# Four buffers for the dense output's transposed tiles, and their logits five planned microseconds later

## The chip, the cores and the metric

The kernel runs on one NeuronCore of a Trainium2 chip. The metric is the device time of one execution in microseconds (us). The core has five engines that each work through a list of their own in order: TensorE (PE, whose weight loads are shown as PEld), VectorE (DVE), ScalarE (ACT), GpSimd (POOL) and SyncE (SP), which issues most of the DMAs.

## What is computed

The reference is a chain of three layers over 3072 tokens (4 batches of 768) with 320 features:

```python
# 1. a recurrent attention over time (4 batches, 8 heads, 768 steps, 40 wide), with stabilised gates
C = f_stab * C + i_stab * outer(v_t, k_t);  n = f_stab * n + i_stab * k_t
y[:, :, t] = sigmoid(o_gate_t) * (C @ q_t) / max(|n . q_t|, 1)
# 2. a dense layer, 320 -> 2048 -> 320
h = x @ w_in;  g = maximum(0.01 * h, h);  x = g @ w_out
# 3. one expert of eight for each token, 320 -> 1024 -> 320
logits = x @ w_gate;  e_idx = argmax(logits)
eom = sigmoid(x @ w_output_gate)
out[mask] = gate_w * eom[e] * (maximum(x[mask] @ w1[e], 0) @ w2[e])
```

## The kernel before

Attention is done in 24 units (6 chunks of 128 time steps by 4 batches). A unit makes one tile of 128 tokens; two units make a pair, so there are 12 pairs. A pair's tokens go through the dense layer in eight steps of `gemm1` (PE line L870, 16 matmuls), an evaluation on three engines (`t` on ACT, `g` on DVE, `gh` on ACT, `gl` on POOL) and, two steps later, `gemm2` (L892 to L894, 12 matmuls). After a pair's last `gemm2`, `finish` copies or adds the accumulators into float32 rows and starts `x2out` for each of the two tiles.

`x2out` is what the change touches. It packs the float32 rows into two float16 halves (`x2r`, by ACT and DVE), writes them to DRAM (`x2rows`, SP line L902), has a DMA transpose them into a tile `x2T` (SP line L904), and then computes the tile's router logits: eight small matmuls `lp<-wg,x2T` (PE, L915) and a copy to `Lall` on ACT. The tiles are numbered 0 to 23; tile i belongs to batch b = i mod 4. Tiles 0 to 19 (pairs 0 to 9, `bufs` given, called part A in the code, `TA = 20`) take this way; the logits of tiles 20 to 23 are kept in `late` and computed later, among the expert blocks. `x2T` has two buffers in the pool `dp`.

The order on each engine is not the order of the code. Every piece of work is a generator that is started at a planned time; `yield 3.0` in `x2out` puts the logits' planned time three microseconds behind that of the transpose. `Order.run` then goes through all instructions with a cost model of its own, gives each engine the ready instruction with the lowest planned time, and fixes that order (for planned times up to 350). So a planned time sets a place in a list, and nothing at run time waits for a clock: at run time an instruction starts when those ahead of it on its engine have started and what it reads is there.

The arena is one large tile that holds other data in each stage. Its region `R3`, 5120 float16 columns, holds `X2F` (float32 rows of the dense output), `YR` (L769's product of queries and state, scaled on DVE and added to `o1` on DVE) and `X32`. Later, the second weight of expert 3 is put into the same columns.

After the dense layer, part A's logits are routed (a long chain on DVE), tokens are gathered into blocks of 128, and the blocks run through the experts (L1177 and L1196) to the end.

Of the kernel before, what the change touches and what calls it, by code (L numbers as in the profile page):

```python
# [9 lines left out]
F16 = mybir.dt.float16  # L10
# [9 lines left out]
B, H, S, D = 4, 8, 768, 40  # L20
# [9 lines left out]
TA = 2 * PF  # L30
# [3 lines left out]
D1 = D + 1  # L34
# [45 lines left out]
class Order:  # L80
# [62 lines left out]
    def run(self, instrs, planned, pools):  # L143
# [57 lines left out]
        def enter(i):  # L201
            q = ops[i]
            t = ready_t[i]
            if q.engine == E.SP:
                t = max(t, prio[i] - DMALEAD)
            heapq.heappush(wait[q.engine], (t, i))
# [6 lines left out]
        while n < len(ops):  # L213
# [11 lines left out]
            if not avail[e]:  # L225
                free[e] = t
                continue
            if e == E.SP and dma_free > t + DMAQ:
                free[e] = dma_free - DMAQ + 0.001
                continue  # L230
# [113 lines left out]

CHAINT = 350
DMALEAD = 2
DMAQ = 10


def emit(tc, gates, qkv, og, w_in, w_out, w_gate, w1, w2, out):  # L350
# [11 lines left out]
    def tt(eng, o, a, b, op):  # L362
        eng.tensor_tensor(out=o, in0=a, in1=b, op=op)  # L363
# [7 lines left out]
    def copy(o, a, s=1.0):  # L371
        A.activation(out=o, in_=a, func=AF.Copy, scale=s)  # L372
# [65 lines left out]
    dp = Slots(tc.alloc_tile_pool(name="dp", bufs=2), 2)  # L438
# [102 lines left out]
    R3 = Region(3 * 5120, 4 * 5120)  # L541
# [11 lines left out]
    CH = Bufs([cp.tile([104, H, 42], F16, name="ch"), R.f16(H, 42, p=104)], "CH")  # L553
    CL = Bufs([R.f16(H, 42, p=104) for _ in range(2)], "CL")
    C3 = [R.f16(H, 42) for _ in range(B)]
    YR = Bufs([R3.f32(H, D1) for _ in range(2)], "YR")
    X32 = Bufs([R3.f32(H, D) for _ in range(2)], "X32")
    SG = Bufs([R.f32(B, DM) for _ in range(2)], "SG")
    for t in CH.items + CL.items:
# [125 lines left out]
    def unit(i):  # L685
# [78 lines left out]
        if c > 0:  # L764
            assert C3[b] is None or ver[b] == c, (i, ver)
            yr = YR()
            o2 = ps.tile([128, H, D1], F32, tag="aux", name="o2", bufs=3)
# [5 lines left out]
            tt(V, o1, o1, yr, ALU.add)  # L773
            YR.free(yr)
        else:
# [61 lines left out]
    def pack(xr, x, s, pool=False):  # L837
        dup = lambda a: a.unsqueeze(1).to_broadcast([128, 2, 64])
        v2 = lambda a: a.rearrange("p (u d) -> p u d", u=2)
        copy(xr[:, 0:256], x[:, 0:256], s)  # L840
        copy(v2(xr[:, 512:640]), dup(x[:, 256:320]), s)
        for o, a, hi in ((xr[:, 256:512], x[:, 0:256], xr[:, 0:256]),
                         (v2(xr[:, 640:768]), dup(x[:, 256:320]), v2(xr[:, 512:640]))):
            if pool:
                less(True, o, a, hi)
            else:
                low(o, a, s, hi)
# [48 lines left out]
    def x2out(acc, c, b, bufs, tag="aux"):  # L896
        i = c * B + b
        xr = dp.tile([128, 768], F16, tag="x2r", name="x2r")
        pack(xr, acc, S_X2 / (S_X * S_WIN * S_WOUT))
        if bufs:  # L900
            bufs.free(acc)
        SP.dma_start(x2rows[i * 128:(i + 1) * 128, :], xr)  # L902
        x2T = dp.tile([128, 6, 128], F16, tag="x2T", name="x2T")
        SP.dma_start_transpose(out=x2T, in_=xr)  # L904
        if bufs:
            yield 3.0
            logits(i, x2T, tag)
        else:
            late.append((i, x2T, tag))

    def logits(i, x2T, tag):
        lp = ps.tile([128, 16], F32, tag=tag, name="lp", bufs=NB[tag])
        with tc.high_priority():
            for m, (xb, wb) in enumerate(X_MOVES):
                T.matmul(lp, x2T[:, xb, :], wg[:, wb, :], start=(m == 0), stop=(m == 7))  # L915
            copy(Lall[:, i, :], lp)
# [345 lines left out]
    def finish(p, kp):  # L1262
        for i in range(2):
            a = acc[p][i]
            if p < 4 and kp == 3:
                if i:
                    V.tensor_copy(part[p][i], a)
                else:
                    copy(part[p][i], a)
                continue  # L1270
            if p < PF:
                x = X2F()
                if p < 4:
                    tt(V, x, a, part[p][i], ALU.add)
                elif i:
                    V.tensor_copy(x, a)
                else:
                    copy(x, a)
                a = x
            at(now + 0.5 + 0.1 * i, x2out(a, *pairs[p][i], X2F if p < PF else None))  # L1280
        del acc[p]
# [94 lines left out]
def build(arrays):  # L1376
    import concourse.bacc as bacc

    nc = bacc.Bacc("TRN2", target_bir_lowering=False, num_devices=1)
    args = [nc.dram_tensor(n, a.shape, mybir.dt.from_np(a.dtype), kind="ExternalInput").ap()  # L1380
            for n, a in arrays.items()]
    args.append(nc.dram_tensor("out", (NT, DM), F32, kind="ExternalOutput").ap())
    with tile.TileContext(nc, schedule_with_timeline_sim=True) as tc:
        emit(tc, *args)
    return nc
# [9 lines left out]
```

## Time and profile before

| what | us |
|---|---|
| median of 3 runs | 690.59 (687.31 to 693.65) |
| the profiled execution's own time | 690.56 |
| its span, first to last instruction | 688.8 |
| PE busy in the span | 618.6 |

The profiled execution is as long as the median run, and 1.8 us of it lie outside the span. An engine's busy time says how much of the span its instructions cover; the idle time in front of an instruction is put down to whatever released it.

### The profile page before, as it was taken

The numbers are of one execution on the slowest core, as the hardware profiler recorded it, in microseconds if no ns is written. First come the engines' busy times: TensorE is split into PE (matmuls) and PEld (weight loads), VectorE is DVE, ScalarE is ACT, GpSimd is POOL, SyncE is SP. The second block draws the span as 40 slices with busy tenths as digits, with TensorE's granted clock in tenths as the row PEclk, the third lists the DMA queues.
The fourth block names the chain that finished last, engine by engine and source line by source line (L and its number), as shares of the span: only waits on it lengthen the run. The fifth ranks groups of instructions, "written<-read, shape, count | busy, mean of one in ns | idle before, by whom it ended". The sixth has DMA issues, their size and how long they took to land. (4 is left out here: it accounts for less than half of the span.)

```text
span 688.8 us, 14711 instructions
## 1 busy us (share of the span) xinstructions
PE 618.6 (90%) x5276; PEld 460.0 (67%) x5276; DVE 396.5 (58%) x766; ACT 353.8 (51%) x736; POOL 316.7 (46%) x342
## 2 busy tenths in 40 slices
PE   3658999888999899989989999999789999999993
PEld 1547687676777787878878877777445655665652
DVE  6795689935575656754757655698435722222220
ACT  4643584598566588685845665654432222222220
POOL 5483796646375555555444542324513522222211
PEclk9995899999999999999999999999999999999997
DMA  8865494763779886997484665734899878868842
GB/s 243 264 159 148 144 255 131 243 186 60 157 190 211 174 224 172 254 201 198 122 172 129 167 168 155 183 109 127 210 198 170 163 158 164 156 138 153 168 95 53
DMA packets 213793, 116.67 MB, mean 169 GB/s; under 512 B 168727, under 2 KB 201239, under 8 KB 213720
## 3 DMA queue, kind: packets, MB, share of 16 engines
q1 hardware_dynamic: 210808, 106.64, 66.5%
q0 software_dynamic: 2912, 9.05, 4.9%
q8 instruction: 47, 0.77, 0.5%
q14 instruction: 26, 0.21, 0.1%
HBM read 64.54 MB, written 9.06 MB: 107 GB/s over the span
## 5 line engine op out<-in xcount | busy, mean ns | idle before, releaser
L870 PE MATMUL hp<-xT,arena 128*128 128x256 f16 x1536 | 192.4, 276 | 2.6 <-DVE g L363 2.1
L363 POOL TENSOR_TENSOR gl<-g,gh 128x512 f16<-128x512 f32 x96 | 122.5, 1276 | 135.4 <-ACT gh L372 133.8
L870 PEld LDWEIGHTS <-arena 128*128 128x128 f16 x1536 | 148.8, 99 | 25.0 <-issue 4.0
L892 PE MATMUL acc<-arena,gh 128*128 128x320 f16 x384 | 115.6, 302 | 3.5 <-ACT arena L372 2.4
L894 PE MATMUL acc<-arena,gl 128*128 128x320 f16 x384 | 115.6, 303 | 2.3 <-POOL gl L363 2.3
L893 PE MATMUL acc<-arena,gh 128*128 128x320 f16 x384 | 115.7, 302 | 0.7 <-POOL arena L363 0.7
L360 DVE SCALAR_TENSOR_TENSOR r<-hp,r 128x512 f16<-128x512 f32 x52 | 35.7, 691 | 110.3 <-ACT r L1183 94.9
L1177 PE MATMUL hp<-arena,xbb 128*128 (+1 forms) x480 | 95.6, 381 | 2.9 <-DVE g L363 1.1
L363 DVE TENSOR_TENSOR g<-hp,t 128x512 f32<-128x512 f32 x96 | 65.7, 685 | 49.1 <-ACT t L372 39.3
L1196 PE MATMUL y<-arena,rT 128*128 (+1 forms) x720 | 90.3, 299 | 2.6 <-DMA rT<-r 2.6
L372 ACT ACTIVATE gh<-g 128x512 f16<-128x512 f32 x96 | 60.0, 625 | 46.7 <-DVE g L363 46.1
L1196 PEld LDWEIGHTS <-rT 128*128 128x128 f16 (+1 forms) x720 | 61.9, 101 | 29.7 <-DMA rT<-r 3.7
L360 DVE SCALAR_TENSOR_TENSOR arena<-stg,arena 128x960 f16<-128x960 f32 (+3 forms) x48 | 59.6, 1244 | 32.0 <-ACT arena L372 30.7
L372 ACT ACTIVATE t<-hp 128x512 f32<-128x512 f32 x96 | 56.3, 586 | 39.1 <-PE hp L870 38.8
L1177 PEld LDWEIGHTS <-xbb 128*128 128x128 f16 (+1 forms) x480 | 41.5, 101 | 47.9 <-issue 4.8
L1200 POOL DMA_INDIRECT out<-ys,si x26 | 26.8, 1033 | 88.4 <-ACT ys L1199 71.9
L372 ACT ACTIVATE arena<-arena 128x640 f16<-128x640 f32 (+4 forms) x73 | 49.2, 688 | 33.6 <-DVE arena L360 14.8
L360 DVE SCALAR_TENSOR_TENSOR arena<-arena 128x320 f16<-128x320 f32 (+4 forms) x64 | 54.6, 860 | 17.3 <-ACT arena L372 16.7
L1183 ACT ACTIVATE r<-hp 128x512 f16<-128x512 f32 x52 | 30.8, 598 | 52.8 <-PE hp L1177 44.3
L372 ACT ACTIVATE arena<-stg 128x1024 f16<-128x1024 f32 (+2 forms) x48 | 46.9, 979 | 19.7 <-DMA stg<-w 17.8
L1199 ACT ACTIVATE ys<-y,ss 128x320 f32<-128x320 f32 x26 | 13.7, 527 | 77.0 <-PE y L1196 68.1
L759 PE MATMUL o<-arena 128*128 128x41 f32 x384 | 52.8, 301 | 0.0
(240 smaller groups left out, 810.3 us busy)
## 6 DMA issues: line engine op xcount, KB each, us to landing
stg<-w SPq DMA_DIRECT2D x24, 512.0 KB
arena<-qkv SPq DMA_DIRECT2D x24, 484.0 KB
arena<-gd SPq DMA_DIRECT2D x18, 512.0 KB
stg<-w SPq DMA_DIRECT2D x16, 480.0 KB
raw<-w_in SPq DMA_DIRECT2D x10, 512.0 KB
arena<-w_out SPq DMA_DIRECT2D x8, 640.0 KB
x2rows<-x2r SPq DMA_DIRECT2D x24, 192.0 KB
arena<-og SPq DMA_DIRECT2D x6, 640.0 KB
```

Of the source, the lines that this page charges most:

```text
L360: eng.scalar_tensor_tensor(out=o, in0=a, scalar=s, in1=b, op0=op0, op1=op1)
L363: eng.tensor_tensor(out=o, in0=a, in1=b, op=op)
L372: A.activation(out=o, in_=a, func=AF.Copy, scale=s)
L759: T.matmul(o1[:, h, :], gm[:, h, :], v[:, h, :], start=True, stop=True)
L870: T.matmul(hp[:, kk, :], win_v[:, j, wb, o:o + 128], xT[:, xb, :], start=(m == 0), stop=(m == 7))
L892: T.matmul(acc[i], gh[:, kk, r], wh, start=(k == lo), stop=False)
L893: T.matmul(acc[i], gh[:, kk, r], wl, start=False, stop=False)
L894: T.matmul(acc[i], gl[:, kk, r], wh, start=False, stop=(k == hi))
L1177: T.matmul(hp[n][r], xT[:, xb, r], W1v[:, e, wb, n * 512:(n + 1) * 512].rearrange("p a b -> p (a b)"), start=(m == 0), stop=(m == 7))
L1183: A.activation(out=r[:, 0, :], in_=hp[n], func=AF.Relu)
L1196: T.matmul(y[r], a[:, r], W2v[:, e, k, m, :].rearrange("p a b -> p (a b)"), start=(k + n == 0), stop=(k == 7 and n == 2))
L1200: G.indirect_dma_start(out=out, out_offset=bass.IndirectOffsetOnAxis(ap=D_[s][1][:, i:i + 1], axis=0), in_=ys, in_offset=None, bounds_chec ...
```

## The change

The logits of tiles 0 to 17 get a planned time 8 us behind the transpose in place of 3 us; tiles 18 and 19, the last pair of part A, keep 3 us. Every tile with an odd batch now takes its transposed tile from two buffers in the arena (`X2T`), the others from the two of the pool, so that there are four in all. To make room in `R3`, `YR` goes from two buffers to one.

```diff
 CHAINT = 350
 DMALEAD = 2
+
+LOGD = 8.0
 DMAQ = 10
...
-    YR = Bufs([R3.f32(H, D1) for _ in range(2)], "YR")
+    YR = Bufs([R3.f32(H, D1)], "YR")
+    X2T = Bufs([R3.f16(6, 128) for _ in range(2)], "X2T")
...
-        x2T = dp.tile([128, 6, 128], F16, tag="x2T", name="x2T")
+        mine = bufs and b % 2
+        x2T = X2T() if mine else dp.tile([128, 6, 128], F16, tag="x2T", name="x2T")
         SP.dma_start_transpose(out=x2T, in_=xr)
         if bufs:
-            yield 3.0
+
+            yield 3.0 if i >= TA - 2 else LOGD
             logits(i, x2T, tag)
+            if mine:
+                X2T.free(x2T)
```

What this does to the order is shown at three places. In the rows, L915 and L922 are the same line before and after (logits); so are L892 to L894 and L895 to L897 (`gemm2`), L870 and L873 (`gemm1`), L751 and L754 (`sc`, a unit's scores), L759 and L762 (`o1`), L769 and L772 (`o2`), L902 and L905 (rows to DRAM), L904 and L908 (the transposes), L722 and L725 (transposes of a unit's queries and keys), L809 to L811 and L812 to L814 (a unit's state).

On PE at tile 12, before: the logits stand inside a `gemm2`, behind its seventh matmul.

```order
L894 LDWEIGHTS gl
L894 MATMUL acc<-arena,gl 128x320
L892 LDWEIGHTS gh
L892 MATMUL acc<-arena,gh 128x320
L915 LDWEIGHTS x2T
L915 MATMUL lp<-wg,x2T 128x16
...
L893 LDWEIGHTS gh
L893 MATMUL acc<-arena,gh 128x320
```

On PE at tile 12, after:

```order
L896 LDWEIGHTS gh
L896 MATMUL acc<-arena,gh 128x320
L897 LDWEIGHTS gl
L897 MATMUL acc<-arena,gl 128x320
L754 LDWEIGHTS arena
L754 MATMUL sc<-arena 128x128
...
L922 LDWEIGHTS x2T
L922 MATMUL lp<-wg,x2T 128x16
...
L873 LDWEIGHTS arena
```

The logits of tile 12 now stand behind the whole `gemm2` (five matmuls more) and behind four score matmuls of a unit.

On SP at tiles 12 and 13, before: the transpose of tile 13 stands behind four state copies.

```order
L902 DMA x2rows<-x2r 128x768
L904 DMA_TRANSPOSE x2T<-x2r 128x6x128
L902 DMA x2rows<-x2r 128x768
L809 DMA arena<-arena 40x336
L810 DMA arena<-arena 40x336
L811 DMA arena<-arena 40x336
L809 DMA arena<-arena 40x336
L904 DMA_TRANSPOSE x2T<-x2r 128x6x128
```

On SP at tiles 12 and 13, after:

```order
L905 DMA x2rows<-x2r 128x768
L908 DMA_TRANSPOSE x2T<-x2r 128x6x128
L905 DMA x2rows<-x2r 128x768
L908 DMA_TRANSPOSE arena<-x2r 128x6x128
L812 DMA arena<-arena 40x336
L813 DMA arena<-arena 40x336
L814 DMA arena<-arena 40x336
L812 DMA arena<-arena 40x336
```

The odd tile's transpose, now into the arena, stands ahead of the state copies.

On PE at tile 0, before: its logits follow the 14th matmul of a `gemm1`.

```order
L870 LDWEIGHTS arena
L870 MATMUL hp<-xT,arena 128x256
L915 LDWEIGHTS x2T
L915 MATMUL lp<-wg,x2T 128x16
...
L870 LDWEIGHTS arena
L870 MATMUL hp<-xT,arena 128x256
...
L892 LDWEIGHTS gh
L892 MATMUL acc<-arena,gh 128x320
```

On PE at tile 0, after:

```order
L897 LDWEIGHTS gl
L897 MATMUL acc<-arena,gl 128x320
L762 MATMUL o_1805<-arena 128x41 x8
L772 LDWEIGHTS arena
L772 MATMUL o_1894<-arena 128x41
...
L922 LDWEIGHTS x2T
L922 MATMUL lp<-wg,x2T 128x16
```

The rest of that `gemm1`, a whole `gemm2` and a unit's `o1` and `o2` now stand ahead of them.

## Rows read from the trace of the kernel before

**Rows 1.** The page: PE's busy time, and the granted clock in 40 slices (tenths).

```profile
PE 618.6 (90%) x5276; PEld 460.0 (67%) x5276; DVE 396.5 (58%) x766; ACT 353.8 (51%) x736; POOL 316.7 (46%) x342
...
PEclk9995899999999999999999999999999999999997
```

**Rows 2.** Busy time by stretch: PE, PEld, DVE, ACT, POOL; clock; DMA share, GB/s.

```profile
160.00:200.00 40.00, 34.96 (x361) 28.48 (x359) 24.73 (x45) 26.63 (x70) 21.99 (x23) 1.00 0.69 152
...
280.00:320.00 40.00, 38.27 (x418) 32.58 (x418) 24.98 (x53) 29.85 (x68) 22.14 (x26) 1.00 0.85 214
...
440.00:480.00 40.00, 38.05 (x332) 29.98 (x331) 34.12 (x79) 20.25 (x34) 14.15 (x11) 1.00 0.45 125
480.00:520.00 40.00, 32.98 (x211) 18.51 (x209) 17.09 (x34) 15.53 (x33) 13.40 (x11) 0.96 0.95 202
```

**Rows 3.** Waits, whole span: us in total, times, longest.

```profile
PE lp L915 <- DMA x2T<-x2r: 14.4, 14, 1.8
...
ACT Lall L372 <- PE lp L915: 7.2, 11, 1.9
```

**Rows 4.** Waits of PE between 160 and 440 us, all of them.

```profile
PE lp L915 <- DMA x2T<-x2r: 13.5, 13, 1.8
PE sc L751 <- DVE arena L363: 2.4, 3, 1.4
PE hp L870 <- DVE g L363: 0.5, 1, 0.5
```

**Rows 5.** Timeline of PE around tile 12's logits: start, us, instruction [idle before].

```profile
344.94 0.30 PE L894 MATMUL acc<-arena,gl 128*128 128x320 f16 x1
345.08 0.30 PE L892 MATMUL acc<-arena,gh 128*128 128x320 f16 x1
...
345.49 0.30 PE L892 MATMUL acc<-arena,gh 128*128 128x320 f16 x1
347.60 0.36 PE L915 MATMUL lp<-wg,x2T 128*128 128x16 f16 x8 [1.81 <-DMA x2T<-x2r]
```

**Rows 6.** Timeline of PE: tile 0's logits, a dense gemm1, a unit's o1.

```profile
168.67 0.36 PE L915 MATMUL lp<-wg,x2T 128*128 128x16 f16 x8 [1.08 <-DMA x2T<-x2r]
...
181.50 1.91 PE L870 MATMUL hp<-xT,arena 128*128 128x256 f16 x16
...
184.88 1.88 PE L759 MATMUL o<-arena 128*128 128x41 f32 x16
```

**Rows 7.** Timeline of SP, the transpose of tile 0.

```profile
165.84 1.25 SPq L904 DMA_TRANSPOSE x2T<-x2r  x1
```

**Rows 8.** Timeline of SP, the transposes of tiles 12 and 13.

```profile
341.70 1.37 SPq L904 DMA_TRANSPOSE x2T<-x2r  x1
343.16 0.55 SPq L902 DMA_DIRECT2D x2rows<-x2r  x1
...
348.11 1.23 SPq L904 DMA_TRANSPOSE x2T<-x2r  x1
```

**Rows 9.** Timeline of POOL, the `gl` of the gemm2 at 344.7 us.

```profile
337.83 1.16 POOL L363 TENSOR_TENSOR gl<-g,gh 128x512 f16<-128x512 f32 x1 [0.80 <-ACT gh L372]
```

**Rows 10.** Busy time by stretch (columns as in group 2), around a clock drop.

```profile
236.00:242.00 6.00, 6.00 (x46) 4.84 (x47) 2.42 (x7) 0.78 (x2) 2.02 (x2) 0.72 0.65 130
342.00:348.00 6.00, 4.19 (x50) 3.29 (x49) 5.55 (x9) 3.26 (x6) 1.40 (x2) 1.00 0.91 196
```

**Rows 11.** Timeline of PE, tile 7's logits and what follows.

```profile
235.63 0.36 PE L915 MATMUL lp<-wg,x2T 128*128 128x16 f16 x8 [0.69 <-DMA x2T<-x2r]
...
237.91 3.35 PE L870 MATMUL hp<-xT,arena 128*128 128x256 f16 x15
```

**Rows 12.** Waits of PE between 440 and 520 us, the longest.

```profile
PE acc L894 <- POOL gl L363: 2.1, 2, 1.8
```

**Rows 13.** Timeline of PE around tile 19's logits.

```profile
442.23 0.60 PE L870 MATMUL hp<-xT,arena 128*128 128x256 f16 x4
443.72 0.36 PE L915 MATMUL lp<-wg,x2T 128*128 128x16 f16 x8 [0.89 <-DMA x2T<-x2r]
```

## Prediction

> **What bounds the kernel now.** I read the page first: PE is busy for 618.6 of 688.8 us, far above any other engine, and its clock is granted in full almost everywhere behind the start [rows 1]. The table of stretches then shows three stages [rows 2]. From 160 to 440 us the dense layer and the attention units share the core, with PE busy for 35 to 39 of each 40 us and DVE and ACT for 25 to 31. From about 445 us DVE's routing chain is the tighter one (34.1 of 40 us). Behind 480 us the expert blocks start with some idle time. A busy PE tells how full it is but not what its idle time is worth, so the third view is the list of waits. Over the whole span its longest row on PE is the router's logits waiting for the DMA that transposes their tile: 14 waits, 14.4 us, the longest 1.8 [rows 3]. Between 160 and 440 us there is hardly anything else: 13 of these waits with 13.5 us, against 2.4 and 0.5 us for the two other reasons [rows 4]. PE takes its matmuls in order, so whatever stands behind the logits waits too.
>
> **The waits, priced.** At tile 12 [rows 5] the `gemm2` matmuls follow each other every 0.14 us (344.94 to 345.08), then the logits come 1.81 us behind the end of the last. The view counts idle time from the end of a matmul, which lasts 0.30 us although the next could have started 0.14 us behind its start. So a wait costs the idle time plus about 0.17 us (0.16 behind `gemm2`; 0.17 behind `gemm1`, whose 16 matmuls take 1.91 us, so 0.11 each [rows 6] with an end 0.28 behind the start). In all: 14.4 + 14 x 0.17 = 16.8 us. Tile 19's wait, 0.89 + 0.16 = 1.05 us [rows 13], belongs to a tile whose planned time stays. **15.75 us** are within the change's reach.
>
> Why they wait: a transpose is not there soon. Tile 0's is issued at 165.84 [rows 7] and its logits start at 168.67 [rows 6], 2.8 us later; tile 12's takes from 341.70 [rows 8] to 347.60 [rows 5], 5.9 us. These are the shortest kind and the longest. [...]
>
> **What the later planned time does.** It does not add 5 us; it moves the logits back in PE's list, and the order shows by how much. I priced the matmuls that now stand between the old place and the new with the spacings above (`gemm1` 0.11, `gemm2` 0.14; a unit's `o1` 1.88 for 16 [rows 6], so 1.7 until the next can start; a unit's scores and `o2` follow one another still closer and make under 0.25 us of any entry). For tiles 0 to 17 this gives 3.8, 4.5, 1.9, 1.4, 0.8, 1.5, 2.6, 1.7, 1.7, 2.6, 2.5, 2.5, 0.9, 0.95, 2.3, 3.0, 1.1 and 1.6 us. The waits to be covered, priced as above, are 1.2, 1.35, 0.8, 0.9, 0.2, 1.0, 1.3, 0.85, 1.9, 0.75, 1.9, 0, 2.0, 0, 0, 0, 0.4 and 1.2 us. Each is covered but two: tile 8 keeps 0.15 and tile 12 keeps 1.1 us. Tile 19's logits come five `gemm1` matmuls earlier in the list (0.55 us), while its transpose comes one SP instruction sooner; I take 0.3 us, between 0 and 0.55.
>
> The two added buffers and the lost one: the transposes of odd tiles write to the arena and stand earlier on SP. At 13 the transpose was issued at 348.11, 4.95 us behind the write of its rows at 343.16 [rows 8], because four state copies stood between; now it goes first and the copies come 1.3 us later (1.23 us of SP, plus a gap). No wait of PE between 160 and 440 us is for a unit's state or for its transposed queries and keys [rows 4], so these had time to spare, how much the list does not tell; I take 0, at most 1.3 us for each of the nine odd tiles below 18. `YR` with one buffer orders the next unit's scaled product behind this unit's addition. Both are on DVE, which takes them in this order anyway: 0. The second expert weight that later lands on `X2T` is converted behind tile 19's logits in both orders: 0.
>
> **Does something else take the waits' place?** What PE waits for next is the evaluation chain (ACT, DVE, ACT, POOL). The `gl` that the `gemm2` at 344.7 us reads ended at 337.83 + 1.16 = 338.99 [rows 9], 5.95 us ahead of its first use at 344.94 [rows 5], and read in the same way, the lead of most other steps is 2 to 7 us. Removing 1 or 2 us ahead of a step eats into that lead but not through it, and the other engines gain too: ACT idles for 7.2 us for these same logits [rows 3]. Behind 440 us everything hangs on what PE has finished (the logits of tile 19 start DVE's routing, the last `gemm2` frees the columns for the last weights), so the whole rest moves forward by what was saved.
>
> Sum: 15.75 - 0.15 - 1.1 - 0.3 = **14.2 us**, against the profiled execution's own 690.56: 676.4. That execution is as long as the median of the three runs (690.59), so no correction: **676 us**.
>
> **The clock.** Once in the stage, just behind tile 7's logits, the granted clock falls to the lower level, 1.2 GHz: the mean from 236 to 242 us is 0.72 [rows 10], and 15 `gemm1` matmuls take 3.35 us [rows 11] where 16 take 1.91. That is 1.6 us. Just ahead of it PE had waited for tile 7's logits (0.69 us) [rows 11]. Around the longest wait, at tile 12, the clock stays at 2.4 GHz (1.00 from 342 to 348 us) [rows 10], so one wait does not bring it on, and I leave the 1.6 us out of the sum and put it into the low end.
>
> **The rivals.**
> - *The moved transposes bite.* SP is a list too: with odd tiles first, the transposes of queries and keys, and the state copies, are issued 1.3 us later. If none of that is covered, PE waits for scores or `o2`: 9 x 1.3 = 11.7 us come back, 688 us. For it: scores already wait three times, 2.4 us. Against: those waits are for DVE, not for a DMA [rows 4].
> - *The stage is paced by DMA, not by PE.* Then PE only gets to the next transfer sooner: about 690 us. For it: a DMA share of 0.85 from 280 to 320 us [rows 2]. Against: in that stage PE waits for no DMA but the logits' [rows 4]. The Trainium skill, in "Perfetto Trace Analysis", section "What "DMA-bound" means", calls a kernel DMA-bound when single DMA engines or the issuing sequencer are at their limit; a mean share of 0.85 over 16 engines neither shows nor excludes that, so this rival keeps a chance.
> - *ACT stops at the copies (slower).* ACT works in order; the copy of the logits to `Lall` now stands elsewhere in its list, and if it stands ahead of the evaluation of a step while PE comes to the logits late, `t` and `gh` are held, and through them `gemm2`. It costs only what exceeds the lead (5.95 us at the step shown). Above 0.8 us beyond the lead at each of the 18 tiles (14.2 / 18) it eats the gain; at 1.3 us it takes 23 us, and the time is 700 us. For it: ACT already idles 11 times for these copies [rows 3]. Against: the order moves the copy together with the matmuls.
> - *It does not do what it says*, since the places in the list move too little. The rows of the order exclude it but for tiles 8 and 12; it is in the sum.
>
> **How the numbers follow.** The forecast has a chance of 0.78, the moved transposes 0.11, the DMA's pace 0.06, ACT's copies 0.05. Low end: 676.4 less 1.6 (clock), less 2 us (the longest wait of PE behind 440 us is 2.1 us [rows 12], in a stretch whose order changes as well), less 1.5 us, half of what the shown runs spread below their median: 671 us. High end: 676.4 plus the same 2 us for the worse, plus 8 of the 11.7 us of the first rival: 686.5 us. A difference of under 1% (6.9 us) is about what a measurement of this kernel cannot tell from no change. Faster by over 1%, below 683.7: the forecast's 0.78 and part of the first rival, 0.80. Within 1%: the rest of the first two rivals, 0.15. Slower: 0.05.
>
> **What would show it.** If right, the row of logits waiting for their DMA shrinks from 14 waits to three or four with under 4 us, PE's other waits between 160 and 440 us stay near 3 us, and tile 19's logits start about 13 us sooner than at 443.72 [rows 13]. If the first rival holds, new PE rows appear for scores or `o2` behind a DMA or DVE. If ACT's copies hold, `gemm2` waits for `gh` or `gl`. I am wrong most cheaply if transposes land even later in the tighter stage, so that 1 us of setback no longer covers tiles 4, 12, 16 and 17.

## The result and the profile after

| | us |
|---|---|
| median of the changed kernel, 20 runs | 682.44 (675.34 to 693.38) |
| median of the kernel before, 20 runs beside them | 687.47 (681.11 to 695.12) |
| ratio, with its 95% interval | 0.9917 (0.9892 to 0.9941) |
| the profiled execution's own time, and its span | 689.69, 688.0 |

The change makes the kernel 5.0 us faster. The forecast was 14 us and a time of 676, so the sign was right, the size was not, and the gain is below the 1% that the forecast gave a chance of 0.80. The forecast's time started from 690.56 us, 3.1 us above the median of the 20 runs before, so it misses the time by 6 us and the gain by 9; that the time looks nearer is luck. The profiled execution of the changed kernel happens to be one of its slow ones (granted clock 0.968 over the span, 0.975 in the one of before), which the ratios here and below leave out, so its own time says nothing on the gain, and stretches are compared with the clock taken out.

First the same list of waits as in [rows 4], PE from 160 to 440 us of the changed kernel: what was waited for, us in total, times, longest.

```profile
PE sc L754 <- DVE arena L365: 8.1, 7, 2.0
PE lp L922 <- DMA arena<-x2r: 2.6, 2, 2.0
PE lp L922 <- DMA x2T<-x2r: 2.6, 3, 1.4
```

The logits' waits fell from 13.5 us to 5.2 (two kinds of row, since odd tiles now read the arena). But the scores' waits rose from 2.4 us to 8.1. These are four matmuls that write the second half of a unit's scores; they need the one PSUM buffer that VectorE has to read first, in its multiply of the first half. Net, PE waits 13.3 us there in place of 16.4.

Where in the kernel the gain is missing is seen by cutting the span at three events that both kernels have: the last `gemm2` matmul of the dense layer's steps 19, 45 and 85 (of 96, counted from 0), and the end of the fifth expert block. First the kernel before, in these cuts; columns are width, busy time of PE, PEld, DVE, ACT and POOL (with counts), granted clock, DMA share, GB/s.

```profile
160.40:290.90 130.50, 119.81 (x1226) 98.73 (x1224) 83.59 (x161) 88.65 (x212) 73.61 (x78) 0.99 0.80 189
290.90:455.30 164.40, 157.63 (x1493) 130.16 (x1492) 103.27 (x176) 106.07 (x210) 73.50 (x73) 1.00 0.66 165
455.30:537.40 82.10, 73.35 (x520) 47.03 (x519) 52.15 (x150) 30.53 (x59) 27.86 (x23) 0.98 0.76 163
```

The changed kernel, between the same events:

```profile
160.20:291.70 131.50, 120.68 (x1226) 100.25 (x1225) 80.42 (x160) 91.60 (x216) 69.74 (x78) 0.97 0.81 192
291.70:451.50 159.80, 157.28 (x1493) 130.23 (x1491) 106.14 (x182) 101.87 (x206) 78.54 (x74) 1.00 0.64 163
451.50:536.30 84.80, 74.83 (x521) 47.84 (x519) 52.88 (x146) 32.36 (x60) 29.39 (x24) 0.94 0.74 163
```

In the second cut the change brings 4.6 us (164.4 to 159.8), as much as was forecast for it. In the first, where ten of the fourteen priced microseconds lay, it brings nothing: 130.5 us became 131.5, and PE idles 10.8 us (131.50 - 120.68) where it idled 10.7. In the third cut 2.7 us are lost, with a granted clock of 0.94 in place of 0.98.

Why PE does not get ahead in the first cut, at one place of the changed kernel (`sc` are a unit's scores, `lp` the logits). PE's timeline:

```profile
174.59 0.35 PE L922 MATMUL lp<-wg,arena 128*128 128x16 f16 x8
174.79 0.38 PE L754 MATMUL sc<-arena 120*128 120x128 f16 x4
175.02 1.15 PE L873 MATMUL hp<-xT,arena 128*128 128x256 f16 x9
178.07 0.38 PE L754 MATMUL sc<-arena 120*128 120x128 f16 x4 [1.91 <-DVE arena L365]
```

The logits of tile 1 run without a wait, 0.20 us ahead of the unit's first score half. Nine matmuls later PE stands at the second half for 1.91 us. DVE and ACT at the same time:

```profile
172.68 0.20 DVE L785 RECIPROCAL rd<-rd 128x8 f32<-128x8 f32 x1
175.93 0.49 DVE L362 SCALAR_TENSOR_TENSOR arena<-arena 128x320 f16<-128x320 f32 x1 [3.04 <-ACT arena L374]
176.34 0.48 DVE L362 SCALAR_TENSOR_TENSOR arena<-o,arena 128x320 f32<-128x320 f32 x1
176.74 0.68 DVE L365 TENSOR_TENSOR g<-hp,t 128x512 f32<-128x512 f32 x1
177.34 0.68 DVE L365 TENSOR_TENSOR arena<-sc,arena 128x512 f32<-128x512 f32 x1
```

```profile
175.16 0.74 ACT L374 ACTIVATE arena<-arena 128x640 f16<-128x640 f32 x1 [3.58 <-DMA arena<-qkv]
```

The multiply that PE needs starts at 177.34, 2.5 us after its scores. DVE had nothing to do for 3.04 us ahead of it, because the instruction at the head of its list needs ACT's copy of another unit's queries, and ACT waited 3.58 us for the load of those. SyncE had issued that load at 171.11, behind a transpose of queries and keys that held it for 2.13 us, most of them a wait for PE's `o1` matmuls:

```profile
168.93 2.13 SPq L725 DMA_TRANSPOSE arena<-arena  x1
171.11 0.58 SPq L694 DMA_DIRECT2D arena<-qkv  x1
```

In the kernel before, the same load was issued at 170.48, the first score half started on PE at 177.67, 2.88 us later than here, and the same multiply at 178.10. So PE came to these scores 2.88 us sooner and found VectorE only 0.76 us sooner. While PE waited for the logits, the units' chain of load, ACT and DVE had time to be done; without those waits PE runs into it here.

A second kind of place, DVE ahead of the 2.01-us wait at 261.04 in the changed kernel:

```profile
254.59 0.69 DVE L365 TENSOR_TENSOR g<-hp,t 128x512 f32<-128x512 f32 x1 [3.15 <-ACT t L374]
...
256.73 1.21 DVE L362 SCALAR_TENSOR_TENSOR arena<-stg,arena 128x960 f16<-128x960 f32 x1
...
260.31 0.68 DVE L365 TENSOR_TENSOR arena<-sc,arena 128x512 f32<-128x512 f32 x1
```

Here no transfer is late. After 254.59 DVE works almost without a pause through eleven more instructions, a weights' piece of 1.21 us among them, until it comes to the multiply at 260.31.

### The profile page after: what moved, and what is told of

It is laid out like the page before. It is cut to its first block, busy times and chain, and to the rows that moved or that the text cites. A ratio compares the mean times of both kernels' runs of the same rounds, so it can differ in the third digit from the quotient of the medians.

```text
span 688.0 us, 14705 instructions
## 1 busy us (share of the span) xinstructions
PE 620.5 (90%) x5276; PEld 462.1 (67%) x5276; DVE 396.6 (58%) x766; ACT 354.2 (51%) x736; POOL 319.0 (46%) x342
## 5 line engine op out<-in xcount | busy, mean ns | idle before, releaser
L873 PE MATMUL hp<-xT,arena 128*128 128x256 f16 x1536 | 191.8, 277 | 1.7 <-DVE g L365 1.5
L365 POOL TENSOR_TENSOR gl<-g,gh 128x512 f16<-128x512 f32 x96 | 127.0, 1322 | 122.7 <-ACT gh L374 109.2
L873 PEld LDWEIGHTS <-arena 128*128 128x128 f16 x1536 | 148.3, 99 | 23.2 <-issue 2.6
L895 PE MATMUL acc<-arena,gh 128*128 128x320 f16 x384 | 116.5, 304 | 2.8 <-ACT arena L374 2.4
L897 PE MATMUL acc<-arena,gl 128*128 128x320 f16 x384 | 115.6, 302 | 1.0 <-POOL gl L365 1.0
L1184 PE MATMUL hp<-arena,xbb 128*128 (+1 forms) x480 | 98.0, 387 | 8.4 <-issue 5.4
L762 PE MATMUL o<-arena 128*128 128x41 f32 x384 | 53.0, 302 | 0.0
L1153 POOL DMA_INDIRECT xbb<-x2rows,gi x26 | 27.8, 1070 | 53.8 <-PE hp L1184 43.5
```

The costliest lines, as they stand in the source:

```text
L762: T.matmul(o1[:, h, :], gm[:, h, :], v[:, h, :], start=True, stop=True)
L873: T.matmul(hp[:, kk, :], win_v[:, j, wb, o:o + 128], xT[:, xb, :], start=(m == 0), stop=(m == 7))
L895: T.matmul(acc[i], gh[:, kk, r], wh, start=(k == lo), stop=False)
L897: T.matmul(acc[i], gl[:, kk, r], wh, start=False, stop=(k == hi))
L1153: G.indirect_dma_start(out=xb, out_offset=None, in_=rows, in_offset=bass.IndirectOffsetOnAxis(ap=gi[:, i:i + 1], axis=0), bounds_check=(TA ...
L1184: T.matmul(hp[n][r], xT[:, xb, r], W1v[:, e, wb, n * 512:(n + 1) * 512].rearrange("p a b -> p (a b)"), start=(m == 0), stop=(m == 7))
```

## The experiments

The kernels stand in four groups, and the kernel before was timed again beside each group; ratios are to those runs. "First cut" and "second cut" are the stretches above, from one profile each; "at full clock" takes off 1.7 us for each stretch of 3.4 us in which the trace shows 1.2 GHz. The first theories: A, the attention units are a second limit close behind the logits; B, the new order at the start of the expert blocks costs what is missing; C, more time at the lower clock.

| kernel | median us (runs) | ratio (95%) | first cut: us, at full clock, PE idle | second cut, at full clock |
|---|---|---|---|---|
| before (profile of the start) | | | 130.5, 128.8, 10.7 | 164.4 |
| changed (profile above) | 682.44 (20) | 0.992 (0.989 to 0.994) | 131.5, 128.1, 10.8 | 159.8 |
| again | 685.32 (12) | 0.994 (0.990 to 0.998) | 130.2, 126.8, 9.9 | 159.6 |
| late_only | 686.78 (12) | 0.994 (0.990 to 0.998) | 132.8, 129.4, 12.4 | 160.4 |
| bufs_only | 688.26 (13) | 0.999 (0.995 to 1.003) | 131.9, 128.5, 10.6 | 163.5 |
| stale | 681.94 (6) | 0.989 (0.984 to 0.995) | 126.6, 124.9, 7.6 | 160.3 |
| after_s2 | 685.44 (12) | 0.999 (0.995 to 1.002) | 134.8, 129.7, 12.8 | 160.5 |
| before_s2 | 691.48 (12) | 1.003 (1.000 to 1.007) | 133.0, 129.6, 11.8 | 165.0 |
| late12 | 689.15 (12) | 1.001 (0.997 to 1.005) | 132.2, 128.8, 11.3 | 160.3 |
| after_l6 | 681.66 (13) | 0.990 (0.987 to 0.993) | 126.5, 126.5, 9.3 | 161.0 |
| after_w | 685.93 (12) | 1.000 (0.997 to 1.004) | 122.8, 122.8, 5.5 | 161.8 |
| before_w | 697.02 (6) | 1.014 (1.008 to 1.020) | 132.1, 127.0, 9.5 | 167.9 |
| after_wl6 | 683.69 (12) | 0.997 (0.993 to 1.001) | 120.2, 120.2, 3.1 | 162.2 |
| after_w55 | 683.39 (12) | 0.996 (0.992 to 1.000) | 126.0, 124.3, 7.0 | 161.8 |
| after_w55l6 | 677.70 (6) | 0.981 (0.974 to 0.988) | 123.0, 121.3, 4.4 | 162.7 |
| before_w55l6 | 695.11 (6) | 1.011 (1.005 to 1.018) | 131.5, 128.1, 10.4 | 166.7 |

The medians of before in the four groups were 689.04 (again to stale), 688.48 (after_s2 to after_l6), 688.28 (after_w to after_wl6) and 687.65.

**again**: the changed kernel once more.

> The changed kernel itself, once more, for a profile that is less disturbed and for runs beside the others. All theories: 0.990 to 0.993 of before. Theory A (the attention units are a second limit close behind the logits: with the waits for transposes gone, PE runs into waits for scores): PE's waits for scores between 160 and 440 us are 5 to 7 us again, against 2.4 before. Theory B (the new order where the expert blocks start costs what is missing): PE's first wait for the expert blocks, at about 486 us, is again over 3 us. Theory C (the clock): the half-clock time of this profile is over 10 us above that of before and the waits are not.

685.32 against 689.04: 3.7 us. With the first result, the change is worth 4 to 5 us. PE waits 8.3 us for scores between 160 and 440 us, more than theory A's 5 to 7, and its wait for the first expert block is 5.3 us, as theory B said.

**late_only**: the kernel before with the later planned time alone; the two old buffers stay.

```diff
-            yield 3.0
+            yield 3.0 if i >= TA - 2 else 8.0
```

> Only the later planned time, with the buffers of before (two for the transposed tiles, two for YR). On PE the logits of tiles 0 to 17 get the same setback as in the changed kernel; from tile 18 on the order is that of before. A: the gain in the dense layer is what it was, about 4 to 6 us, so 0.992 of before, with waits for scores of 5 to 7 us. B: the same gain without the loss at the expert blocks, 10 to 12 us in all, 0.984. C: no difference from the changed kernel, 0.992.

2.3 us faster than before, ratio 0.994 where theory B asked for 0.984. In the first cut nothing is gained here either (129.4 us at full clock against 128.8), without the two added buffers and with the order of before at the expert blocks.

**bufs_only**: the changed kernel with the logits at three planned microseconds, so the buffers and the moved transposes alone.

```diff
-LOGD = 8.0
+LOGD = 3.0
```

> Only the buffers (four for the transposed tiles, one YR); the logits keep the 3 us. The order at the expert blocks is close to the changed kernel's. A: the waits for transposes stay at 12 to 16 us and the time is that of before, 1.00. B: slower than before by 4 to 6 us, 1.007. C: 1.00.

No change that can be measured: the moved transposes of odd tiles cost nothing by themselves, and bring nothing.

**stale**: as bufs_only, but the logits read the transposed tile of two tiles earlier, which is always there.

```diff
-            logits(i, x2T, tag)
-            if mine:
-                X2T.free(x2T)
+            kept[i] = x2T
+            logits(i, kept[i - 2] if 2 <= i < TA - 2 else x2T, tag)
+            if mine and i - 2 in kept:
+                X2T.free(kept[i - 2])
...
+    kept = {}
```

> The buffers of the change, 3 us planned, but the logits of tiles 2 to 17 read the transposed tile of two tiles earlier, which landed long ago, so that they wait for nothing; the router then sees wrong tokens for these tiles (about as evenly spread over experts). It measures what the waits of 14 tiles are worth on PE. My prediction's price: these waits are 13 us, so 0.981 without a loss at the expert blocks, 0.988 with one of 5 us. A: PE's waits for scores (or for the evaluation) rise to 6 us or more and the gain by 440 us is under 8 us. B: they stay under 3.5 us and PE is 12 to 14 us earlier at 440 us.

Sixteen tiles' waits are gone by force, and the gain is 7.1 us, not 14. PE's waits from 160 to 440 us in this kernel:

```profile
PE sc L754 <- DVE arena L365: 5.4, 5, 1.8
PE lp L923 <- DMA x2T<-x2r: 2.9, 2, 1.8
```

Nobody waits for a transpose but the tiles whose logits were left as they are, and the score waits still came up from 2.4 to 5.4 us. The router sees wrong tokens here, so the expert blocks do not compare; in the first two cuts this kernel gains 3.9 and 4.1 us at full clock. So even logits that wait for nothing would not have brought the forecast's ten microseconds in the first cut: what fell short is not the price of a wait but what stands behind it.

**after_s2** and **before_s2**: the second score half 2 planned us later in every unit from the ninth on, in the changed kernel and in the one before.

```diff
-        dict(q=11.84, t=18.88, e=11.68, w=14.4, v=15, s0=18.4, s1=19.84, p=25.2, c=25.92, k=27.52, x=27.8, u=32.8, g=0),
+        dict(q=11.84, t=18.88, e=11.68, w=14.4, v=15, s0=18.4, s1=21.84, p=25.2, c=25.92, k=27.52, x=27.8, u=32.8, g=0),
```

> The changed kernel with one planned time of the attention units moved: the second half of a unit's scores 2 planned us later (21.84 in place of 19.84 after the unit's start), from unit 8 on. In the profile of the changed kernel taken beside this run's predecessors TensorE waited 8.3 us (7 waits) for the first half's multiply on VectorE before it could write the second half's scores, against 2.4 us (3 waits) in the kernel before. Theory A (this second limit took the logits waits' place): those waits fall to under 3 us in 155 to 445 us, the half-clock stretches that began at them go too, and the time falls by 5 to 8 us, to 677 to 681 us where the changed kernel has 685. Theory B (the start of the expert blocks costs the rest) and theory C (the clock alone): the score waits may fall, the end does not move, 684 to 687 us.

> The same move of the second score half, in the kernel before, logits at 3 planned us. Theory A: there are only 2.4 us of score waits to win, and the logits waits (14.4 us) stay in front, so 686.5 to 689 us against 689 for the kernel before. If the move is worth the same without the later logits (a gain of its own that has nothing to do with this change): 681 to 684 us.

A miss for theory A as I had put it, in both kernels. The kernel before with this shift took 691.48 us, 2.5 above its range, with 17.2 us of logits' waits. In the changed kernel the score waits fell only to 5.1 us, and the logits' waits came back:

```profile
PE lp L922 <- DMA arena<-x2r: 6.9, 2, 3.6
PE sc L754 <- DVE arena L365: 5.1, 3, 2.1
PE lp L922 <- DMA x2T<-x2r: 3.6, 4, 1.3
```

Moving PE's work about moves the waits about; at full clock the first cut takes 129.7 us in one and 129.6 in the other. I took this to mean that the stretch is held not by the place of the scores in PE's list but by how soon the other engines deliver; the next runs test it.

**late12**: logits 12 planned us behind the transpose.

```diff
-LOGD = 8.0
+LOGD = 12.0
```

> The changed kernel with the logits 12 planned us after the transpose in place of 8. Theory A: the logits waits left in 155 to 445 us (4.0 us, 4 waits) fall to under 1.5 us, the score waits grow by about as much, and the time stays at that of the changed kernel within 2 us, 683 to 687 us. If what was missing from the forecast were only the logits waits that a setback of 5 us is too short for: 3 to 5 us faster than the changed kernel, 680 to 682 us.

Not faster: 689.15 us, a ratio of 1.001 where the changed kernel has 0.992 and 0.994, and 2 us above what theory A allowed. So it is not that a setback of 5 us is merely too short. PE waits 6.9 us for scores and 6.2 for logits from 160 to 440 us, so the logits' waits did not fall as I had expected but rose.

**after_l6**: the loads of q, k and v issued 6 planned us before their unit, from the ninth unit on.

```diff
-DMALEAD = 2
+DMALEAD, LEAD = 2, 6.0
...
-        raw = raw_r()
-        SP.dma_start(raw, qkv[c, b])
+        SP.dma_start(raw := raw_r(), qkv[c, b])
+        if i >= 8: yield LEAD
...
-        at(t if i < 8 else tick(t), unit(i))
+        at(t if i < 8 else tick(t) - LEAD, unit(i))
```

> The changed kernel with the loads of q, k and v issued 6 planned us before their unit starts (from unit 8 on), so that on SyncE they stand ahead of the pair's transposes; everything else of a unit keeps its planned time. A form of theory A in which the second limit is this load: ScalarE's wait for it at 173 to 177 us (3.9 us) goes, the score wait of 2.2 us at 180 us goes with the half-clock stretch that began there, and others of its kind; 680 to 683 us. If the second limit is VectorE's and ScalarE's own queue of work (as at 210 and 262 us, where both are busy without a gap for 5 us before the late multiply), only the wait at 180 us changes, 683.5 to 686 us.

681.66, 6.8 us under before. The wait of PE at 178 us is gone; those of the second kind stay, 2.3 us at 259 us among them. This put theory A into a sharper form: what holds the first cut is the work of ACT and DVE there, and the loads that they wait for.

**after_w** and **before_w**: the nine pieces of the second weights of experts 0 to 2 planned later, in the changed kernel and in the one before. The first cut held seven of them in the changed kernel and eight before, and now holds none. A piece is a load that SyncE issues, a copy on ACT and a subtraction on DVE.

```diff
-LATER = 31.5
+LATER = 60
...
-            u += 3.3
+            u += 0.84
```

> The changed kernel with the expert weights' pieces taken out of the attention units' time: the nine pieces of the second weights of experts 0 to 2, planned 3.3 steps apart from step 31.5, stand 0.84 steps apart from step 60, and those after them follow. Each piece is a load on SyncE, a 128x960 copy on ScalarE (1.0 us) and a 128x960 subtraction on VectorE (1.1 to 1.3 us). Between the last product of step 19 and that of step 45 the changed kernel took 130.2 us (126.8 counted at full clock, 9.9 of it TensorE idle), the kernel before 130.5 (128.8, 10.7). Theory A in its sharper form (there the units' own work on VectorE and ScalarE is the second limit, and the waits only change their place): that stretch falls to 122 to 125 us at full clock with at most 8 us idle, and the time to 679 to 683 us. Rival (the units' order and the transfers set that stretch, whatever else the two engines do): 126 to 128 us, 684 to 687.

> The same move of the weights' pieces in the kernel before. Theory A: the logits still wait for their transposes there, so the stretch from step 19 to step 45 stays at 127.5 to 129 us at full clock and the time at 686 to 690 us. If the pieces are in the way by themselves, whatever the logits do: the stretch and the time fall as much as in the changed kernel with the same move, by 3 to 5 us.

This is the pair that tells the theories apart. The changed kernel with the move:

```profile
160.60:283.40 122.80, 117.33 (x1226) 98.50 (x1224) 74.41 (x154) 86.11 (x209) 68.77 (x78) 1.00 0.78 173
283.40:445.20 161.80, 157.80 (x1493) 130.18 (x1491) 107.58 (x185) 103.46 (x208) 74.33 (x73) 1.00 0.69 175
445.20:535.20 90.00, 74.95 (x520) 47.95 (x518) 53.20 (x139) 35.36 (x64) 26.32 (x24) 0.94 0.75 170
```

The kernel before with the same move:

```profile
155.20:287.30 132.10, 122.59 (x1226) 100.72 (x1224) 74.04 (x152) 82.55 (x199) 68.92 (x78) 0.96 0.73 161
287.30:456.90 169.60, 159.74 (x1493) 130.55 (x1491) 111.69 (x181) 108.11 (x219) 72.43 (x72) 0.99 0.68 168
```

In both, VectorE has 6.0 and 9.5 us less to do in the first cut than without the move (74.4 and 74.0 us in place of 80.4 and 83.6). With the later logits that is worth 4.0 to 5.3 us at full clock (126.8 and 128.1 to 122.8); with the early ones 1.8 us (128.8 to 127.0), because PE still stands at the logits there. The whole times did not follow the expectations, though. In the changed kernel the pieces had gone to the start of the expert blocks, and the third cut grew from 84.8 to 90.0 us. The kernel before took 697.02 us, 7 above its range: at full clock its second cut grew by 3.5 us and its third by 3.3 (80.4 to 83.7).

**after_wl6**: both moves in the changed kernel.

> Both moves in the changed kernel: the weights' pieces out of the units' time, and the loads of q, k and v 6 planned us earlier. Theory A: the two take away different waits (VectorE's backlog, the load's delay), so the stretch from step 19 to step 45 falls below that of either, to 121 to 124 us at full clock, and the time to 676 to 680 us. Rival (order and transfers set the stretch): not below the run with the early loads alone, 681 to 685 us.

The first cut falls to 120.2 us with 3.1 us of idle time, below either move alone, as theory A said; the third cut again gives it back (87.9 us), so the time misses the expectation by 4 us.

**after_w55**, **after_w55l6** and **before_w55l6**: the nine pieces start at step 55, so that all later ones keep their places.

```diff
-LATER = 31.5
+LATER = 55
...
-            u += 3.3
+            u += 0.84
```

> The changed kernel with the nine pieces of the second weights of experts 0 to 2 planned 0.84 steps apart from step 55 (they stood 3.3 steps apart from step 31.5, and from step 60 in the run that crowded the expert blocks); the next pieces begin at step 62.56, as they did. Theory A: the stretch from step 19 to step 45 falls to 122 to 125 us at full clock (126.8 in the changed kernel), the next to step 85 stays at 159.5 to 162, the start of the expert blocks at 80 to 82, and the time falls to 679 to 683 us. Rival (the pieces' place costs the same wherever they stand): 684 to 687 us.

> As the run before, with the loads of q, k and v 6 planned us earlier as well. Theory A: 120 to 122.5 us at full clock from step 19 to step 45, 159.5 to 162 to step 85, 80 to 82 in the next, and 675 to 680 us, what the change alone was forecast to bring. Rival: 682 to 686 us.

> Both moves in the kernel before. Theory A: the logits, which wait for their transposes there, stay the first limit, so the stretch from step 19 to step 45 is 126 to 128 us at full clock (128.8 before) and the time 685 to 688 us. If the moves are worth the same without the later logits: 679 to 682 us, and the later logits are worth no more beside them than by themselves.

after_w55 alone came 0.4 us above its range in time and kept its first cut (124.3 us). Neither move alone makes the whole kernel clearly faster than the changed one: the ratios are 0.996 with the pieces moved and 0.990 with the early loads, beside 0.992 and 0.994. With both:

```profile
158.50:281.50 123.00, 118.64 (x1226) 99.47 (x1225) 74.62 (x154) 86.28 (x208) 66.98 (x76) 0.99 0.77 173
281.50:444.20 162.70, 157.29 (x1492) 130.44 (x1490) 111.32 (x187) 104.97 (x211) 78.11 (x72) 1.00 0.72 181
444.20:527.50 83.30, 72.89 (x521) 47.06 (x520) 53.62 (x146) 32.99 (x61) 30.27 (x24) 0.96 0.78 166
```

This is the fastest kernel of the study: 677.70 us, 10 us under before and ratio 0.981. The kernel before with the same two moves is 7.5 us slower than without them, and its waits from 160 to 440 us show what it stands at:

```profile
PE lp L915 <- DMA x2T<-x2r: 14.5, 13, 2.5
PE acc L894 <- POOL gl L363: 2.0, 1, 2.0
PE sc L751 <- DVE arena L363: 1.5, 2, 1.3
```

The logits wait as long as ever (13.5 us in [rows 4]), and at full clock its first cut is nearly unchanged, 128.1 us where 128.8 was. So in the first cut the later logits are worth 0.7 and 2.0 us by themselves and 6.8 us (128.1 to 121.3) once the other work is out of the way. Over the whole kernel the two are 4 to 5 us and 17.4 (695.11 to 677.70), but the 17.4 also holds the 7.5 us that the two moves cost the kernel before. About 4 of these are lower clock (19.0 us lost per run where 15.0 were, worked out as in the part on the clock below). The price that I had missed besides is in its second cut, 166.7 us at full clock where 164.4 was: more loads fall there (172 GB/s in place of 165), and three waits for a transpose between 389 and 447 us are 1.5 to 2.4 us long. With the clock's loss taken off each run, 13.6 of the 17.4 us are left.

## Why the prediction was wrong, point by point

**What bounds the kernel: half right.** PE was the fullest engine and the logits its longest row of waits. But a row of waits tells what is waited for last; the engines behind were not asked how far behind they were.

**"Does something else take the waits' place?" is the step that failed.** It said that what PE waits for next is the evaluation chain, and measured a lead of 5.95 us on that chain [rows 5, 9]. In the changed kernel the evaluation never became late between 160 and 440 us. The units' scores did: their row stood in [rows 4] with 2.4 us, which means that this chain had a lead of zero at three places already. I read the row as small when it should have been read as next. PE's waits in the first cut, in the kernel before:

```profile
PE lp L915 <- DMA x2T<-x2r: 8.7, 9, 1.7
PE sc L751 <- DVE arena L363: 2.0, 2, 1.4
```

And in the changed kernel:

```profile
PE sc L754 <- DVE arena L365: 7.4, 5, 2.0
PE lp L922 <- DMA arena<-x2r: 2.6, 2, 2.0
PE lp L922 <- DMA x2T<-x2r: 0.8, 1, 0.8
```

Priced as in the prediction, with 0.17 us for each wait, the logits' waits of this cut were worth 10.25 us. 3.9 us of them stayed, where 0.15 was forecast, and 5.9 us more of waits for scores came. By this sum 0.45 us is left of the 10.1 us forecast; measured were 0.7 and 2.0 at full clock in two profiles. Tile 19's logits started at 439.38 us, 4.3 us sooner than before and not 13. The pair before_w and after_w, and the last three runs, show that the units' chain was the next limit: with the weights' pieces moved and the loads brought forward, PE waits only 1.3 us for scores in this cut, and the same change brings 6.8 us there; what stands out then is one wait of 2.0 us for the evaluation. Not shown is which part of the units' chain counts most, since a piece's move takes work from SyncE, ACT and DVE at once.

**The kept waits were sized too small.** Forecast: tile 8 with 0.15, tile 12 with 1.1, tile 19 with 0.3, together 1.55 us. Measured idle time: tiles 6, 7, 9, 12 and 18 with 0.77, 0.64, 1.99, 0.37 and 1.43 us, which with 0.17 each makes 6.05. The prediction named this as the cheapest way to be wrong, but for other tiles. The sum took it that a transpose lands as soon as before; tile 9's logits started 6.2 us behind the issue of their transpose (274.33 to 280.51), before it was 4.1 us (274.71 to 278.76). A longer setback alone does not cure it: in late12 tiles 6 and 12 no longer wait, but tiles 7, 9 and 18 wait 1.55, 2.98 and 1.65 us. With the pieces out of the first cut these waits fell there from 3.4 to 1.0 us (after_w), so they may hang on the same work; no run shows that by itself. Tile 12 in the changed kernel answers to [rows 5]:

```profile
345.69 0.39 PE L754 MATMUL sc<-arena 120*128 120x128 f16 x4
346.45 0.36 PE L922 MATMUL lp<-wg,x2T 128*128 128x16 f16 x8 [0.37 <-DMA x2T<-x2r]
```

0.37 us in place of 1.81, behind four score matmuls that hold the next one up by 0.23 us (174.79 to 175.02 above), as the prediction had put it.

**The pricing of a wait was right.** In the second cut four waits and the kept ones made a forecast of 4.1 us; measured 4.6 and 4.8. Which tiles keep a wait was forecast less well: tile 12 kept 0.5 us in place of 1.1, tile 18 1.6 in place of none, and tile 19 lost all of its 1.05. That these nearly cancel is luck.

**The moved transposes, one buffer less for `YR`: right.** bufs_only shows no cost. The first rival (they bite) named the symptom, scores that wait for DVE, but not the cause: late_only has 8.1 us of the same waits without the two buffers that let the odd transposes go first.

**The two other rivals.** "ACT stops at the copies" did not hold: no wait for `gh` or `gl` stands among PE's from 160 to 440 us. "Paced by DMA" is not excluded for the first cut. PE waits for no DMA there but the logits', yet ACT, on which VectorE's multiply of the scores hangs, waits for loads (3.58 us above), and the move of the pieces also lowers the DMA's rate there from 192 to 173 GB/s. No run takes transfers away alone.

**"Behind 440 us the whole rest moves forward": right at full clock, not in time.** The third cut took 82.1 us before and 84.8 and 83.1 in two profiles of the changed kernel; without the lower clock 80.4, 79.7 and 81.4. The 2 us for a wait in that stretch were misread, too: 2.1 us in [rows 12] are two waits together, and the longest is 1.8. PE's two longest waits there in the changed kernel are new ones:

```profile
PE hp L1184 <- issue: 4.6, 1, 4.6
PE hp L1184 <- DVE x2r L362: 2.9, 1, 2.9
```

The first expert block now stands ahead of the last pieces of `gemm2` on PE and waits for its gathered tokens (its first weights for 3.36 us, for the DMA that transposes those tokens); before, that `gemm2` and its waits came first. late_only, which keeps the order of before there, took 83.1 us as well, so theory B is not where the time went.

**The clock: left out of the sum, and not settled.** The time lost to the lower level, worked out for each run as (1 - granted clock) x span, was 15.9 us on average in the changed kernel's 20 runs (3.4 to 3.7 us of such a sum lie at the end of the span, where PE has no matmul left and the clock is at 0.50); in the 12 of again it was 18.1, and 15.2 in the 29 of the kernel before beside them. So theory C may hold 1 to 3 us of what is missing, but the two sets of the changed kernel differ as much from each other. With this loss taken off each run, the means of again and of the kernel before beside it are 667.2 and 673.9 us: without the clock the change is worth 6.7 us, still half of the forecast. In the same way late_only is worth 2.9 us, so the later time brings more with the four buffers than without them.

## What to carry to other kernels

A wait that is removed brings only the distance to the next limit. Look for that in the list of waits itself: any other reason with even a few waits in the same stretch is a chain whose lead is already used up at those places, and the price of the removed waits must be held against its lead, event by event, not against the lead of the chain that one has in mind. When a change brings less than it should, take load from the suspected second chain in both kernels: if that helps the new kernel much more than the old one, the two changes belong together.

## What the runs showed of the hardware

Run to run, the time follows the granted clock. The fastest of the changed kernel's 20 runs had 0.985 and 675.34 us, the slowest 0.966 and 693.38; over the 104 runs of the kernel before in the four groups, 0.989 and 679.96, 0.964 and 696.76. That is a spread of 18 and 17 us in one and the same program.

The longest stretch at the half clock, 1.2 GHz, stands near the start, where the change has not acted yet. In the kernel before it begins at 53.4 us, at the end of a wait of PE of 4.76 us for VectorE, and lasts 20.5 us; from 57 to 73 us PE is busy without a gap and the clock stays at 0.50. In the 16 profiles this stretch is 6.8 to 23.9 us long. In before_w, which is the same kernel up to there, it lasts 6.8 us, and the first cut begins at 155.2 us in place of 160.4: about 5 us of the spread come from this one place.

Behind 160 us the half clock comes in stretches of 3.4 us, at times two on end, and several of them follow a wait. Two in the changed kernel, each with the stretch ahead of it (the scores' wait of 2.01 us and the logits' of 1.99 lie in the first and third row):

```profile
258.00:261.40 3.40, 1.39 (x16) 1.12 (x14) 3.33 (x9) 3.39 (x8) 1.88 (x2) 1.00 0.49 114
261.40:264.80 3.40, 3.40 (x17) 2.11 (x15) 2.42 (x6) 2.97 (x9) 2.17 (x3) 0.50 0.16 43
...
278.00:281.90 3.90, 1.91 (x46) 1.51 (x44) 2.19 (x3) 2.73 (x8) 1.45 (x2) 1.00 1.22 229
281.90:285.20 3.30, 3.30 (x17) 2.26 (x17) 0.51 (x2) 3.27 (x6) 1.77 (x4) 0.50 1.15 324
```

PE was busy 1.39 of 3.40 and 1.91 of 3.90 us, and then the clock was 0.50. Not every such wait brings it on: at 178 us PE waited 1.91 us and the clock stayed. And a shorter one can stand ahead of it: in the kernel before the clock fell behind a wait of 0.69 us at tile 7 and not behind the 1.81 us at tile 12 [rows 10, 11]. The Trainium skill, in "TensorE: Matmul & The Clock Gate", section "HAM oscillation — how this bites in real kernels", describes a kernel in which each wait of TensorE for a DMA puts the clock back, so that the work behind it starts slow. The order of events at the two places above agrees with it; the waits at 178 us and at tile 12, behind which the clock stayed, show that not every wait of this kernel does so. Whether the changed kernel's fewer and longer waits are why its clock was lower in again is not shown; no run here separates it.
